# Value-weight products of a fused attention and mixture kernel, moved from one pair of PSUM banks to another

## The chip, the cores and the metric

One core of a Trainium2 chip runs the whole kernel. The metric is device microseconds (us) for one execution of the kernel, median of several runs; lower is better.

## What is computed

Three stages feed each other.

```python
# 1. Nystrom attention: 4 batches, 8 heads, 576 tokens, 64 wide, 32 landmarks
A  = softmax(q @ k_lm.T / 8); Bm = softmax(q_lm @ k_lm.T / 8); C = softmax(q_lm @ k.T / 8)
Z  = iterated inverse of Bm (6 steps Z = 2 Z - Z Bm Z)
x  = A @ Z @ C @ v                       # 2304 tokens x 512
# 2. gated feed-forward, 512 -> 1536 -> 512
xn = x / rms(x) * g
x  = (silu(xn @ w_gate) * (xn @ w_val)) @ w_out
# 3. mixture of 8 experts, one per token, 512 -> 1024 -> 512, on tokens with x @ w_skip > 0
out = x + gate * (relu(x @ w1[e]) @ w2[e])
```

## The kernel before

The attention's result is never formed. `A @ (Z C v)` has only 32 landmark rows per head between `A` and the rest, so the kernel multiplies the small matrix `Z C v` (with the norm's scale, held as `WT`) into the feed-forward's weights first. These products, tiles `P`, are what the change touches: for each batch there are six, the gate's (`g`) and the value's (`v`) weights in three column thirds q = 0, 1, 2. Below (g,1) means the gate's product of third 1. The feed-forward then multiplies `P` with `ap_t` (the attention weights `A`, scaled by the norm).

The tokens go in eight units u = 0 to 7, two halves of each of the four batches. In `run_unit` a unit has twelve blocks f = 0 to 11, each six matmuls `pg` (gate) and six `pv` (value), then 144 matmuls `o` with `w_out`. Blocks 0 to 3 use third 0 of `P`, 4 to 7 third 1, 8 to 11 third 2. `hidden_g` and `hidden_v` turn a block into `h_t`: tanh on ScalarE (ACT), two multiplications on VectorE (DVE), a cast on ACT, and a subtraction on GpSimd (POOL).

Beside a unit, other work is threaded in as Python generators: the next batch's attention (`attention`, `group`: tiles `pb`, `sq`, `cT`, `sk`, small `pv` per group of four heads, then the inverse with tiles `nr`, then `gram`, `sq`, `ms`), its preparation (`prep`: tiles `ap`, `ap_t`, after the norm `rbs`), the products (`products`, `product`), and the last unit's output and routing (`finish`: tiles `lp`, `lg`, `x2t`). The program is then handed to a scheduler, which fixes one order for each engine in advance, using its own estimates of durations and of which buffer is free when. On the chip each engine runs its order strictly, waiting on semaphores.

PSUM has eight banks of 128 x 512 floats in three pools: `acc` has four (`pg`, `pv`, `o`), `pa` has two with the tag `a` (after the first batch, all of the attention takes its banks here, through `atbank`), `pb` has two with the tag `b` (through `bank`: the products and everything of `finish`).

`product` (line 821) takes two banks, runs sixteen matmuls into them, and `rsplit` empties each: one cast on ACT and one subtraction on DVE per bank. The weights come back from HBM in `load_w` (line 781): four transfers of 256 KB per product, issued on SyncE's queue (SP). The gate's land in two buffers `wl`, the value's in two buffers `wr`, so the transfers for the next third wait until the product of the third before has read its buffers:

```python
        for n in "gv":
            product(b, q, n)
            ...
            elif n == "g" and q < NQ - 1:
                load_w(n, q + 1)
```

Of the kernel before, what the change touches and what calls it, by code (L numbers as in the profile page):

```python
# [6 lines left out]
F32 = mybir.dt.float32  # L7
# [55 lines left out]
def attention_moe_kernel(  # L63
# [13 lines left out]
    def pool(stack, name, bufs=1, **kw):  # L77
        return stack.enter_context(tc.tile_pool(name=name, bufs=bufs, **kw))

    def rsplit(lo_eng, hi, lo, src):  # L80

        A.copy(hi, src)
        lo_eng.tensor_tensor(lo, src, hi.bitcast(F32), ALU.subtract)
# [28 lines left out]
    pa = pool(ph1, "pa", bufs=2, space=PSUM)  # L112
# [29 lines left out]
    def bank(name):  # L142
        return pb.tile([128, 512], F32, name=name, tag="b")
# [661 lines left out]
    def ptile(n, g, q):  # L805
        i = PIECES.index((n, g))
        return P_t[q][:, i, 0], P_t[q][:, i, 1]
# [13 lines left out]
    def product(b, q, n):  # L821

        pss = [bank("P") for g in range(2)]
        ws = wparts.pop((n, q))

        with tc.manual_schedule(engines={nc.tensor.engine}):
            for c in (1, 0):  # L830
                for i in range(KC):
                    for g in (1, 0):
                        gs = slice(64 * g, 64 * g + 64)
                        PE.matmul(
                            pss[g][32 * i : 32 * i + 32, PC * c : PC * c + PC],
                            WTs[b][gs, i], ws[c][gs, i], start=True, stop=True,
                        )
        for g, ps in enumerate(pss):
            hi, lo = ptile(n, g, q)
            rsplit(V, hi, lo, ps)  # L840

    def products(b, q):

        if b == 0:
            for n, g in PIECES:
                product0(q, n, g)
                yield
            return
        last = b == B - 1 and q == NQ - 1
        for n in "g" if last else "gv":  # L850
            if (n, q) not in wparts:
                load_w(n, q)
        for n in "gv":
            product(b, q, n)
            if last and n == "g":
                load_w("v", q, last)
                yield
            elif n == "g" and q < NQ - 1:
                load_w(n, q + 1)
            yield  # L860
# [555 lines left out]
```

## Time and profile before

| | us |
|---|---|
| median of 3 runs (711.12 to 711.80) | 711.46 |
| the profiled execution | 710.12 |
| its span, first to last instruction | 708.4 |
| TensorE busy (PE) in the span | 650.1 (92%) |
| VectorE busy (DVE) | 459.8 (65%) |
| ScalarE busy (ACT) | 295.4 (42%) |
| GpSimd busy (POOL) | 145.1 (20%) |

The profiled execution's time lies 1.72 us over its span and 1.34 us under the median. A busy PE is not PE at its peak: the ends of matmuls are modelled, and a stretch at half the granted clock counts as busy too. Sixteen matmuls of a product stand as 32 rows of the trace (`x32`), since each plain float32 matmul leaves two rows; `pg`, `pv` and `o` leave one each. The time after about 500 us is the last unit and the mixture of experts.

### The profile page before, as it was taken

The page shows a single profiled execution, that of the slowest core. Times are in us where ns is not written, and L with a number is a line of the kernel's source. Part 1 is how long each engine was busy: PE and PEld are TensorE (multiplying, and loading weights), DVE is VectorE, ACT ScalarE, POOL GpSimd, SP SyncE. Part 2 cuts the span into 40 slices and gives each one's busy share as a digit, 9 for nine tenths or more (in the row PEclk, how much of TensorE's full clock was granted, in tenths as well). Part 3 has the DMA queues.
Part 4 walks back from the last instruction along what each step waited for, and adds up shares of the span by engine and source line. Part 5 has one row for each costly group of instructions (what it writes and reads, how often), then busy time and mean ns, then how long its engine had stood idle before and what let it go on. Part 6 is the DMA issues. An engine that isn't in the chain of part 4 may idle for free.

```text
span 708.4 us, 13179 instructions
## 1 busy us (share of the span) xinstructions
PE 650.1 (92%) x4895; PEld 561.1 (79%) x4895; DVE 459.8 (65%) x1030; ACT 295.4 (42%) x637; POOL 145.1 (20%) x162
## 2 busy tenths in 40 slices
PE   5368599798998899999999999999989999999997
PEld 5256177687986598978899887999889988988985
DVE  5995999979877596878368768261452554352451
ACT  0873888834324431443341335240452244242340
POOL 4000035213200140220040030040372024022120
PEclk9775799999998999999999999999999999999999
DMA  8686644762238543428522108230451275445454
GB/s 295 229 256 223 218 148 160 215 171 83 67 95 182 123 111 86 132 64 201 134 66 68 66 20 170 67 73 1 161 153 64 60 234 197 150 130 175 134 158 147
DMA packets 79439, 97.17 MB, mean 137 GB/s; under 512 B 16016, under 2 KB 58000, under 8 KB 79376
## 3 DMA queue, kind: packets, MB, share of 16 engines
q1 hardware_dynamic: 79376, 96.33, 46.2%
q8 instruction: 39, 0.64, 0.4%
q14 instruction: 24, 0.20, 0.1%
HBM read 76.97 MB, written 19.34 MB: 136 GB/s over the span
## 4 chain that ended last, share of the span: by engine, by line
PE 70%; DVE 16%; DMA 4%; ACT 3%; issue 3%; POOL 2%; SPq 1%; POOLq 0%; ACTq 0%; DVEq 0%
PE o L58 17%; PE py L58 11%; PE ph L58 11%; PE pv L58 9%; PE pg L58 8%; PE P L58 3%; PE sq L58 3%; DVE wo L58 3%; PE nr L58 2%; DVE h L58 2%; DVE rbs L58 2%; DVE P L58 1%; PE sk L58 1%; DMA kq<-in_q_dram 1%; DVE ap L58 1%
## 5 line engine op out<-in xcount | busy, mean ns | idle before, releaser
L58 PE MATMUL o<-h_t,wo 128*128 128x288 f32 x1152 | 168.1, 301 | 6.5 <-ACT wo L58 3.6
L58 PEld LDWEIGHTS o<-h_t,wo 128*128 128x128 f32 x1152 | 157.3, 190 | 15.5 <-issue 5.9
L58 POOL TENSOR_TENSOR h_t<-h,h_t 128x288 fp32r<-128x288 f32 x96 | 81.6, 853 | 366.1 <-ACT h_t L58 343.8
L58 PE MATMUL pg<-ap_t,P 128*128 128x288 f32 x576 | 101.1, 305 | 10.8 <-ACT P L58 7.9
L58 PE MATMUL pv<-ap_t,P 128*128 128x288 f32 x576 | 102.4, 306 | 2.5 <-DVE h L58 2.1
L58 PEld LDWEIGHTS pg<-ap_t,P 128*128 128x128 f32 x576 | 83.1, 190 | 22.9 <-issue 14.8
L58 PEld LDWEIGHTS pv<-ap_t,P 128*128 128x128 f32 x576 | 83.8, 191 | 8.7 <-DVE h L58 4.3
L58 PE MATMUL ph<-xsh,P 128*128 128x288 f32 x384 | 78.1, 296 | 0.0
L58 DVE SCALAR_TENSOR_TENSOR h<-h,pg 128x288 f32<-128x288 f32 x96 | 42.6, 446 | 33.8 <-ACT h L58 33.2
L58 PEld LDWEIGHTS ph<-xsh,P 128*128 128x128 f32 x384 | 62.0, 188 | 0.6 <-issue 0.5
L58 ACT ACTIVATE h<-pg 128x288 f32<-128x288 f32 x96 | 39.2, 410 | 49.1 <-PE pg L58 46.4
L58 PE MATMUL ph<-xsl,P 128*128 128x288 f32 x192 | 56.9, 296 | 0.0
L58 ACT CAST h_t<-h 128x288 fp32r<-128x288 f32 x96 | 41.2, 431 | 30.2 <-DVE h L58 29.7
L58 PE MATMUL py<-wo,h_t 128*128 128x512 f32 x210 | 51.7, 397 | 0.0
L58 DVE TENSOR_TENSOR h<-h,pv 128x288 f32<-128x288 f32 x96 | 42.5, 446 | 7.7 <-PE pv L58 5.0
L58 PEld LDWEIGHTS py<-wo,h_t 128*128 128x128 f32 x210 | 39.5, 188 | 9.6
L58 DVE STREAM_TRANSPOSE T<-kq 64x576 f32<-64x576 f32 (+1 forms) x40 | 35.5, 887 | 5.1 <-DMA kq<-in_k_dram 4.0
L58 PEld LDWEIGHTS ph<-xsl,P 128*128 128x128 f32 x192 | 36.0, 188 | 0.1
L58 DVE TENSOR_TENSOR P<-P,P 128x512 fp32r<-128x512 f32 x48 | 31.6, 681 | 6.8 <-ACT P L58 6.5
L58 POOL TENSOR_TENSOR P<-w1r,P 128x512 fp32r<-128x512 f32 x16 | 21.2, 1329 | 69.0 <-ACT P L58 66.9
L58 ACT CAST P<-P 128x512 fp32r<-128x512 f32 x48 | 26.3, 587 | 21.7 <-PE P L58 21.1
L58 DVE TENSOR_SCALAR x2T<-o 128x288 f32<-128x288 f32 x16 | 7.3, 456 | 40.6 <-PE o L58 40.5
(235 smaller groups left out, 954.5 us busy)
## 6 DMA issues: line engine op xcount, KB each, us to landing
wl<-wg_d SPq DMA_DIRECT2D x36, 256.0 KB, 4.6
wr<-wv_d SPq DMA_DIRECT2D x32, 256.0 KB, 4.9
w1r<-in_moe_w_dram SPq DMA_DIRECT2D x32, 256.0 KB, 3.3
wr<-in_moe_w_gate_dram SPq DMA_DIRECT2D x6, 1024.0 KB, 6.3
wr<-in_moe_w_val_dram SPq DMA_DIRECT2D x6, 1024.0 KB, 5.9
wo<-in_moe_w_dram SPq DMA_DIRECT2D x24, 256.0 KB, 5.0
kq<-in_k_dram SPq DMA_DIRECT2D x8, 576.0 KB, 4.4
kq<-in_q_dram SPq DMA_DIRECT2D x8, 576.0 KB, 4.1
```

The source lines that it names most:

```text
L58: return f(*args, **kw)
```

## The change

In `product` the value's two banks now come from `pa`, the pool that the attention uses; the gate's still come from `pb`.

```diff
-        pss = [bank("P") for g in range(2)]
+
+        if n == "g":
+            pss = [bank("P") for g in range(2)]
+        else:
+            pss = [pa.tile([128, 512], F32, name="P", tag="a") for g in range(2)]
```

No instruction is added or removed; the scheduler lays the orders out anew, and they differ from the first product of batch 1 (near the end of unit 1) up to unit 6. In the orders below `P<-wl` is a gate's product, `P<-wr` a value's, and `x16` its sixteen matmuls.

The first place is TensorE from the end of unit 1 into unit 2, before:

```order
L58 MATMUL P<-wl,WT 32x256 x16
L58 MATMUL o<-h_t,wo 128x288 x54
L58 MATMUL pg<-ap_t,P_675 128x288
L58 MATMUL P<-wl,WT 32x256 x16
L58 MATMUL pg<-ap_t,P_675 128x288 x5
L58 MATMUL P<-wr,WT 32x256 x16
L58 MATMUL pb<-lmk_2544,bdq 64x32 x2
L58 MATMUL sq<-T,bdq 64x288
L58 MATMUL pv<-ap_t,P_675 128x288 x2
L58 MATMUL pg<-ap_t,P_675 128x288 x5
L58 MATMUL pv<-ap_t,P_675 128x288 x4
```

and with the change:

```order
L58 MATMUL P<-wl,WT 32x256 x16
L58 MATMUL o<-h_t,wo 128x288 x6
L58 MATMUL P<-wr,WT 32x256 x16
L58 MATMUL o<-h_t,wo 128x288 x33
L58 MATMUL P<-wl,WT 32x256 x16
L58 MATMUL o<-h_t,wo 128x288 x15
L58 MATMUL pg<-ap_t,P_675 128x288 x6
L58 MATMUL pv<-ap_t,P_675 128x288 x6
L58 MATMUL pg<-ap_t,P_675 128x288 x6
L58 MATMUL P<-wr,WT 32x256 x16
L58 MATMUL pv<-ap_t,P_675 128x288 x6
```

The product (v,0), which `pv` of block 0 needs, stood after (g,1) and after `pg` of block 0; now it follows (g,0) at once. The attention of batch 2 (`pb`, `sq` and so on), whose first group stood in blocks 0 to 7 of unit 2, now starts in the `o` part of that unit.

The second place is TensorE from unit 3 into unit 4, before:

```order
L58 MATMUL P<-wr,WT 32x256
L58 MATMUL pv<-ap_t,P_984 128x288 x5
L58 MATMUL o<-h_t,wo 128x288 x3
L58 MATMUL P<-wr,WT 32x256 x15
L58 MATMUL o<-h_t,wo 128x288 x28
L58 MATMUL P<-wl,WT 32x256
L58 MATMUL o<-h_t,wo 128x288 x8
L58 MATMUL P<-wl,WT 32x256 x15
L58 MATMUL o<-h_t,wo 128x288 x17
L58 MATMUL P<-wr,WT 32x256
L58 MATMUL o<-h_t,wo 128x288
L58 MATMUL P<-wr,WT 32x256 x15
```

and with the change:

```order
L58 MATMUL pg<-ap_t,P_984 128x288 x4
L58 MATMUL pv<-ap_t,P_984 128x288 x6
L58 MATMUL o<-h_t,wo 128x288 x5
L58 MATMUL ms<-sq,onesd 128x288 x2
L58 MATMUL o<-h_t,wo 128x288 x6
L58 MATMUL P<-wr,WT 32x256 x16
L58 MATMUL o<-h_t,wo 128x288 x4
L58 MATMUL P<-wl,WT 32x256 x16
L58 MATMUL o<-h_t,wo 128x288 x46
L58 MATMUL P<-wr,WT 32x256 x16
```

Products that were cut into one matmul and fifteen now stand whole, and (g,1) follows (v,0) after 4 `o` matmuls in place of 28.

The third place is TensorE from unit 5 into unit 6, before:

```order
L58 MATMUL P<-wr,WT 32x256
L58 MATMUL pg<-ap_t,P_984 128x288 x6
L58 MATMUL pv<-ap_t,P_984 128x288 x2
L58 MATMUL P<-wr,WT 32x256 x15
L58 MATMUL pv<-ap_t,P_984 128x288 x4
L58 MATMUL o<-h_t,wo 128x288 x24
L58 MATMUL P<-wl,WT 32x256
L58 MATMUL o<-h_t,wo 128x288 x7
L58 MATMUL P<-wl,WT 32x256 x15
```

and with the change:

```order
L58 MATMUL pg<-ap_t,P_984 128x288 x3
L58 MATMUL P<-wr,WT 32x256 x16
L58 MATMUL pg<-ap_t,P_984 128x288 x3
L58 MATMUL pv<-ap_t,P_984 128x288 x6
L58 MATMUL o<-h_t,wo 128x288 x16
L58 MATMUL P<-wl,WT 32x256 x16
```

Here too the products stand whole, and (g,1) comes eight `o` matmuls earlier.

## Rows read from the trace of the kernel before

**Rows 1.** Engine busy time by stretch: PE, PEld, DVE, ACT, POOL; granted clock; DMA share, GB/s.

```profile
210.00:220.00 10.00, 8.92 (x90) 7.98 (x89) 9.97 (x17) 4.48 (x10) 0.00 (x0) 1.00 0.59 145
220.00:230.00 10.00, 8.72 (x64) 6.39 (x65) 6.03 (x18) 3.17 (x8) 0.81 (x1) 0.66 1.02 220
230.00:240.00 10.00, 8.85 (x102) 4.89 (x100) 3.23 (x8) 3.92 (x11) 0.81 (x1) 1.00 0.53 116
240.00:250.00 10.00, 8.66 (x107) 6.74 (x107) 9.32 (x22) 4.53 (x14) 1.85 (x2) 1.00 0.48 112
250.00:260.00 10.00, 9.93 (x92) 9.44 (x91) 8.71 (x27) 4.72 (x13) 5.12 (x6) 1.00 0.32 91
```

**Rows 2.** Timeline of PE, units 1 to 2: start, duration, instruction, idle time before it.

```profile
208.42 1.09 PE L58 MATMUL P<-wl,WT 64*32 64x256 f32 x32
...
220.71 2.20 PE L58 MATMUL P<-wr,WT 64*32 64x256 f32 x32 [1.78 <-DVE P L58]
...
236.64 0.62 PE L58 MATMUL P<-wl,WT 64*32 64x256 f32 x2 [0.67 <-DVE P L58]
...
241.79 1.74 PE L58 MATMUL P<-wr,WT 64*32 64x256 f32 x32
...
246.72 0.77 PE L58 MATMUL lg<-ident,h 128*128 128x9 f32 x6 [1.02 <-DVE P L58]
```

**Rows 3.** PE by stretches of one us: busy, granted clock, DMA share, GB/s.

```profile
136.00:137.00 1.00, 1.00 (x7) 0.71 0.14 53
...
139.00:140.00 1.00, 1.00 (x6) 0.59 0.54 169
...
215.00:216.00 1.00, 1.00 (x10) 1.00 0.27 51
...
221.00:222.00 1.00, 1.00 (x25) 0.87 1.00 294
...
228.00:229.00 1.00, 1.00 (x7) 0.71 1.18 226
```

**Rows 4.** Timeline of PE in unit 0.

```profile
124.58 2.22 PE L58 MATMUL o<-h_t,wo 128*128 128x288 f32 x14 [1.46 <-ACT wo L58]
...
135.05 6.04 PE L58 MATMUL o<-h_t,wo 128*128 128x288 f32 x32 [1.79 <-POOL wo L58]
```

**Rows 5.** Timeline of DVE, units 1 to 2.

```profile
208.83 3.76 DVE L58 RECIPROCAL rbs<-rbs 128x288 f32<-128x288 f32 x2
...
219.97 1.28 DVE L58 TENSOR_TENSOR P<-P,P 128x512 fp32r<-128x512 f32 x2
...
222.04 0.44 DVE L58 SCALAR_TENSOR_TENSOR h<-h,pg 128x288 f32<-128x288 f32 x1
```

**Rows 6.** The chain of work that ended last, in order of time: start, us, what.

```profile
230.75 0.80 PE pg L58 x6
...
260.61 15.18 PE o L58 x114
...
344.62 1.02 PE P L58 x32
...
427.92 7.11 DMA wl<-wg_d
...
478.85 19.19 PE o L58 x144
```

**Rows 7.** Timeline of PE, units 3 to 4 and 5 to 6.

```profile
314.19 1.08 PE L58 MATMUL P<-wl,WT 64*32 64x256 f32 x28
...
323.65 0.62 PE L58 MATMUL P<-wl,WT 64*32 64x256 f32 x2
...
425.20 1.08 PE L58 MATMUL P<-wl,WT 64*32 64x256 f32 x28
...
435.16 0.59 PE L58 MATMUL P<-wl,WT 64*32 64x256 f32 x2 [0.45 <-DMA wl<-wg_d]
```

**Rows 8.** Timeline of SP, unit 1: issue of the gate's weights for third 1.

```profile
209.18 3.30 SPq L793 DMA_DIRECT2D wl<-wg_d  x4
```

## The prediction

> **What bounds the kernel now.** I read the busy times first, by stretches. From unit 1 to the end TensorE is the engine that is hardly ever free, so the time is what TensorE has to do plus what it waits or runs slowly. The table by stretches shows where that is: between 210 and 260 us PE is busy 8.92, 8.72, 8.85, 8.66 and 9.93 of 10 us, so it idles 4.9 us there [rows 1]. In the same place the granted clock falls to 0.66 over ten microseconds [rows 1], and VectorE is busy 9.97 of 10 us just before [rows 1].
>
> Then the timeline of PE, to see what it waited for. At 220.71 it starts a value's product after 1.78 us idle, released by DVE emptying a P bank; at 236.64 again, 0.67 us; at 246.72 the routing's `lg` waits 1.02 us for the same kind of bank [rows 2]. So in this place six products and the last unit's output queue for two banks. DVE cannot empty them sooner: from 208.83 it is held by a reciprocal of 3.76 us [rows 5].
>
> After the longest of these waits the clock falls: 0.87 in the us from 221, 0.71 in that from 228 [rows 3]. Read as full speed and half (2.4 and 1.2 GHz), that is half speed from about 221.7 to 228.6, 6.8 us. In unit 0, two idle times close together, the second of 1.79 us [rows 4], are followed by half speed from about 136.4 to 139.8 [rows 3], while a single one of 1.46 us [rows 4] was followed by none. A half-speed stretch costs half of what PE works in it: about 1.7 us for the short one and 3.1 for the long one, less its idle half microsecond.
>
> **The change, part by part.** No instruction comes or goes. At full speed a block half takes 0.80 us [rows 6], a whole product 1.02 [rows 6], an `o` matmul 19.19 / 144 = 0.133 [rows 6], before and after. Only waits, clock and the cutting of products can change.
>
> *Place one, units 1 to 2.* What can be won there: idle 4.9, half speed 3.1, a product stretched by a wait inside it, 1.74 - 1.02 = 0.7, and one cut product, whose single first matmul holds PE 0.62 [rows 2] where a two-row share of 1.02 would be 0.06: 0.55. Together 9.3 us.
>
> What comes in place: (v,0) is now ready when block 0 needs it, so the wait of 1.78 goes. Next late are three things. First, the weights of (g,1). The new order comes to that product after 6 + 33 `o` matmuls and one product: 209.5 (the end of the first product in [rows 2]) + 5.2 + 1.0 = 215.7. SP issues its four transfers from 209.18 to 212.48 [rows 8], and the DMA's share falls to 0.27 in the us from 215 [rows 3], so they have landed at 215.3 when alone; the value's transfers now follow on SP at once and share the DMA. I take 1.2 us of wait (bounds 0 and 2.6; the upper one from the 7.11 us of a shared transfer [rows 6], counted from the last issue, 211.7). Second, VectorE. The first multiplication of `h` stood at 222.04 [rows 5]; now the value's two subtractions, 1.28 us [rows 5], and about 0.5 of landmark sums go ahead of it, so it comes at about 223.9. PE, two blocks ahead by its four `acc` banks, then waits about 1.0 for the block after, since four more subtractions of 0.64 stand between. Third, `lp`, `lg` and `x2t` still share the gate's two banks: 1.7, the larger part of two evacuations, and 0.6 at block 7. Sum of the three: 4.5. Place one gives 9.3 - 4.5 = 4.8. Bounds: 3.1 if VectorE makes all the waits as long as now and only the clock comes back; 8.1 if only the weights' wait remains. The attention group moved into the `o` part of unit 2 costs PE the same there; its DVE work leaves the crowded stretch with it, and if it did not, the 3.3 us of waits on VectorE counted above (1.0, 1.7 and 0.6) would about double.
>
> *Place two, units 3 to 4.* Four products that were cut stand whole: 4 x 0.55 = 2.2 won (one of the four is the 0.62 in [rows 7]). But (g,1) comes earlier: after (g,0), which ends at 315.3 [rows 7], stand 25 `pg`, `pv` and `o` matmuls (3.3), one product and two short `ms`: 5.2 us, where before it was 8.4 (323.65 [rows 7], without a wait). Weights land 5.8 us after the end of (g,0) in place one (215.3 - 209.5) and at most 8.4 here, so PE waits 0.6 to 3.2; I take 1.7, nearer the lower end since the first two transfers can start sooner. Place two gives 0.5 (bounds -1.0 and 1.6).
>
> *Place three, units 5 to 6.* Here PE waited for the weights already, 0.45 us [rows 7], for a transfer of 7.11 us that landed at 435.03 [rows 6]. Eight `o` matmuls (1.1) and a cut product (0.55) leave the way before it, so PE is there at 434.7 - 1.65 = 433.1 and waits 1.9, or 2.7 if the value's transfers, now started sooner, slow it; I take 2.2, that is 1.75 more, less 1.1 for two products that stand whole: -0.7 (bounds -1.5 and 0).
>
> *The clock.* A wait of about 2 us is longer than the one that was followed by half speed [rows 2, 3]. I count one new short half-speed stretch, most likely at place three: -1.7 (bounds 0 and three long ones, 9).
>
> The TensorE page of the Trainium skill (TensorE: Matmul & The Clock Gate, section on a second failure mode, depth-cycling of the PSUM queue) says that many short idles between matmul groups that cycle through banks make the clock swing. By that rule the waits that remain at place one would bring half speed too, 1.7 to 3.1 us, and the time would be 710 to 712. The trace does not bear it out there: between 230 and 250 us PE waited 0.67 and 1.02 us [rows 2] at a granted clock of 1.00 [rows 1].
>
> Sum: 4.8 + 0.5 - 0.7 - 1.7 = 2.9 us less. The profiled execution took 710.12, so 707.2; it stood 1.34 under the median, so 708.6.
>
> **The rivals.**
>
> *VectorE sets place one.* The banks are not the reason, only the place where a full VectorE is felt. For it: 9.97 of 10 us before the stall and the 3.76 us of reciprocals [rows 1, 5]. Against it: in the twenty microseconds of the stall DVE is busy 6.03 and 3.23 of 10 [rows 1]; it waits for PE as much as PE for it. Then place one gives the clock alone, 3.1, less 0.7 and 1.7, and with 0.5: 711.46 - 1.2 = 710.3, or up to 712 with bounds of the other places. The Trainium skill, Perfetto Trace Analysis, section on the most-contended engine, says that VectorE's busy share tells how near it is to its limit and that the most contended engine is the one to relieve. By that rule, with 9.97 of 10 at the start, more banks win nothing; the row shows it for one stretch of ten microseconds and not for the two in which PE waits.
>
> *Half speed at place one as well.* The 4.5 us of waits that remain there come in four pieces within some fifteen microseconds; two idle times close together were enough in unit 0 [rows 3, 4]. That is 1.7 to 3.1 us on top of the sum: 710.3 to 711.7. Against it: the waits of 0.67 and 1.02 us after 230, at full speed [rows 1, 2].
>
> *The weights become the bound (slower).* One mechanism at all three places: with free banks the scheduler puts (g,1) right behind (v,0), before its transfers can have landed. At the upper bounds PE waits 2.6, 3.2 and 2.7 us in place of the 1.2, 1.7 and 2.2 of the sum: 3.4 more; and half speed follows each, three times 1.7 to 3.1 in place of one time 1.7: 3.4 to 7.6 more. That is 715.4 to 719.6. It decides, that is the sum turns negative, when the waits reach about 2.5 us at two places and the clock falls after both. For it: transfers of 7.11 us have been seen [rows 6]. Against it: four of them alone were there 6.1 us after the first issue [rows 3, 8].
>
> *No new half speed, weights nearly in time.* Then 4.8 to 8.1 at place one, and 0 to 1 at the others: 703 to 707.
>
> *The banks of `pa` are taken when the value's products need them.* The attention uses them, so `P` could wait there for `ms` or `sq`. The new order puts (v,0) after `ms`, whose banks are emptied by a short step; I give this little. The time would stay at 711.5.
>
> **How the numbers follow.** A measurement of this kernel can tell about 0.2%, 1.4 us, from no change. Chances: my sum with one new half-speed stretch (706.5 to 710.5) 0.42; no new half speed (703 to 707) 0.22; VectorE, or waits in `pa` (710 to 712.8) 0.14; half speed at place one as well (710.3 to 711.7) 0.07; the weights' waits with half speed at two places or more (712.5 and above) 0.15. Faster than 710.0: 0.40 of the first, all of the second and 0.02 of VectorE's, 0.64; within 0.2%: 0.22; slower: 0.14. The range leaves out the tail of the weights' case above 713 and of the best case below 704: 704.0 to 713.0. Cases of both signs do not share the chance evenly; the likeliest one's own range is 706.5 to 710.5.
>
> **What would show it.** In the changed kernel's profile the `P<-wr` of unit 1 should start without a wait near 210 us, and `pv` of block 0 follow `pg` at once; PE should idle under 4 us between 210 and 250, at a granted clock of 1.00. Near the two later passages, about 5 us after a gate's product ends, a wait of PE `P` for DMA `wl` of 1 to 3 us should stand, and perhaps half speed behind it. The unit's `o` part should start about 13 us earlier in unit 2, of which 5 are the attention group that moved behind. Wrong would be: an idle time at 220 us as long as before (VectorE), no wait for `wl` at all (then the gain is larger), or half speed behind every wait (then it is slower).

## The result and the profile after

The changed kernel takes 703.55 us (median of 11 executions, 699.17 to 706.69); the kernel before, on the same chip, 711.12 us (median of 11, 706.74 to 712.82). The ratio is 0.9891 with an interval of 0.9869 to 0.9912: 7.6 us less. The forecast was 708.6, with 704.0 to 713.0 as its range: right in sign, less than half of the gain, and the time lies 0.45 us under the range. Executions of one kernel differ by about 1% here, so single times below carry little; ratios do.

| us | before | after |
|---|---|---|
| profiled execution | 710.12 | 704.67 |
| span | 708.4 | 702.8 |
| PE busy | 650.1 | 643.6 |
| DVE busy | 459.8 | 459.7 |
| start of (g,0), batch 1 | 208.42 | 211.00 |
| from that start to the end of (g,0), batch 2 | 106.85 | 100.56 |
| from that end to the end of (g,0), batch 3 | 111.01 | 110.35 |
| from that end to the end of the span | 282.12 | 280.89 |

Up to 208 us the two programs are the same; that this stretch took 2.6 us longer in the profile after is the spread between executions. From the first changed product on, the changed kernel needs 8.2 us less: 6.3 around place one, 0.7 around place two, 1.2 around place three and after it. The two small shares are no larger than what these stretches differ by between executions: the middle one took 109.6 us when the change was run again, and the last one 281.5 and 283.8 us in two experiments that keep all the banks of before.

Over place one PE's busy time (then its granted clock, DMA share, GB/s) is, before and after:

```profile
208.42:315.27 106.85, 101.94 (x940) 0.97 0.46 116
211.00:311.55 100.55, 96.38 (x939) 1.00 0.48 117
```

So only 0.7 of the 6.3 us is idle time, 4.9 to 4.2. The other 5.6 are matmuls that take less time: by the prediction's working 3.1 of it is the half speed that is gone, and the products' own busy time falls from 11.2 to 8.6 us, partly by the clock and partly because they stand whole.

The stretches that answer to [rows 1], in the same columns:

```profile
210.00:220.00 10.00, 8.98 (x118) 7.22 (x124) 9.49 (x14) 4.05 (x8) 0.00 (x0) 1.00 0.73 153
220.00:230.00 10.00, 9.92 (x121) 8.54 (x110) 9.31 (x24) 5.77 (x11) 0.81 (x1) 1.00 1.13 245
230.00:240.00 10.00, 7.73 (x101) 5.82 (x109) 5.38 (x14) 4.07 (x12) 2.05 (x3) 1.00 0.57 139
240.00:250.00 10.00, 9.21 (x87) 8.57 (x65) 7.66 (x22) 4.88 (x12) 4.35 (x6) 1.00 0.44 101
```

The clock of 0.66 is gone; it is 1.00 throughout. PE still idles about 4.2 us from 210 to 250, a little over the 4 that the prediction named as a sign. But VectorE, at 9.49 and 9.31 of 10 us where it was 9.97 and 6.03, now works through the stretch in which it stood waiting before. What PE waits for stands in its timeline (the rows that answer to [rows 2, 7]):

```profile
211.00 1.09 PE L58 MATMUL P<-wl,WT 64*32 64x256 f32 x32
213.02 1.09 PE L58 MATMUL P<-wr,WT 64*32 64x256 f32 x32
219.73 1.22 PE L58 MATMUL P<-wl,WT 64*32 64x256 f32 x32 [1.02 <-DVE P L58]
...
230.24 1.06 PE L58 MATMUL pv<-ap_t,P 128*128 128x288 f32 x6 [0.32 <-DVE h L58]
...
233.78 0.69 PE L58 MATMUL lp<-x2T,wcat 128*32 128x288 f32 x8 [1.46 <-DVE P L58]
235.05 0.77 PE L58 MATMUL lg<-ident,h 128*128 128x9 f32 x6 [0.57 <-ACT h L58]
...
243.97 1.07 PE L58 MATMUL pg<-ap_t,P 128*128 128x288 f32 x6 [0.79 <-DVE h L58]
...
310.90 0.66 PE L58 MATMUL P<-wl,WT 64*32 64x256 f32 x14
...
318.72 1.10 PE L58 MATMUL P<-wl,WT 64*32 64x256 f32 x32 [1.14 <-DMA wl<-wg_d]
...
420.83 1.08 PE L58 MATMUL P<-wl,WT 64*32 64x256 f32 x28
...
429.39 1.22 PE L58 MATMUL P<-wl,WT 64*32 64x256 f32 x32 [0.69 <-DMA wl<-wg_d]
```

At 213.02 the value's product (v,0) follows without a wait where it stood at 220.71 after 1.78 us of idle time [rows 2]. The waits that remain at place one add up to 1.02 + 0.32 + 1.46 + 0.57 + 0.79 = 4.16 us; places two and three have the waits for the gate's weights that were forecast, shorter.

The wait of 1.02 us before (g,1) is put down to VectorE emptying a `P` bank. What VectorE had just emptied were the value's banks, which (g,1) doesn't use. It had done with the gate's at 217.66 (timeline of DVE in the changed kernel, first line below), and when the change was run again the same wait was put down to the weights (timeline of PE in that run, second line). So it is read here as the wait for the weights that was forecast.

```profile
216.98 0.68 DVE L58 TENSOR_TENSOR P<-P,P 128x512 fp32r<-128x512 f32 x1
...
218.40 1.22 PE L58 MATMUL P<-wl,WT 64*32 64x256 f32 x32 [1.45 <-DMA wl<-wg_d]
```

### The profile page after: what moved, and what is told of

Read it like the earlier page. It is cut to its first block, busy times and chain, and to the rows that moved or that the text cites. A ratio compares the mean times of both kernels' runs of the same rounds, so it can differ in the third digit from the quotient of the medians.

```text
span 702.8 us, 13190 instructions
## 1 busy us (share of the span) xinstructions
PE 643.6 (92%) x4895; PEld 559.6 (80%) x4895; DVE 459.7 (65%) x1030; ACT 296.5 (42%) x637; POOL 145.1 (21%) x162
## 4 chain that ended last, share of the span: by engine, by line
PE 72%; DVE 15%; ACT 4%; DMA 3%; issue 3%; POOL 1%; SPq 1%; POOLq 0%; ACTq 0%; DVEq 0%
PE o L58 18%; PE py L58 11%; PE ph L58 11%; PE pv L58 9%; PE pg L58 8%; PE sq L58 3%; PE P L58 3%; DVE wo L58 2%; DVE h L58 2%; DVE rbs L58 2%; DVE P L58 2%; PE nr L58 2%; PE sk L58 2%; DMA kq<-in_q_dram 1%; DVE ap L58 1%
## 5 line engine op out<-in xcount | busy, mean ns | idle before, releaser
L58 PE MATMUL pv<-ap_t,P 128*128 128x288 f32 x576 | 100.5, 303 | 3.5 <-DVE h L58 3.0
L58 DVE SCALAR_TENSOR_TENSOR h_t<-ph,h_t 128x288 fp32r<-128x288 f32 (+2 forms) x45 | 14.6, 352 | 28.4 <-ACT h_t L58 28.4
```

The costliest lines, as they stand in the source:

```text
L58: return f(*args, **kw)
```

## The experiments

**Where the gain is: batch 1 alone.** The value's products take the attention's banks for batch 1 only, which is place one.

```diff
-        if n == "g":
+        if n == "g" or b != 1:
```

> The value's products use the attention's banks for batch 1 alone; batches 2 and 3 keep the shared pair. The orders are those of the change up to unit 2, and close to those of before from unit 4 on. If place one holds nearly all of the gain (6.3 of 8.2 us by the traces from the first product of batch 1 on), this is 5 to 7 us faster than before, ratio 0.990 to 0.993, and the passages from unit 3 to 4 and 5 to 6 take 27.7 and 28.4 us as before. If the gain is spread over the places as products that stand whole, it is about a third: 2 to 3 us, ratio 0.996 to 0.997.

Measured: 704.8 us (median), ratio 0.9921 (0.9893 to 0.9948). The stretch at place one takes 100.62 us, against 100.56 with the whole change. So most of the gain is place one: 5.6 of 7.7 us by the ratios, whose intervals overlap. In its timeline of PE the waits there are those of the change, that of `lp` for one:

```profile
231.58 0.69 PE L58 MATMUL lp<-x2T,wcat 128*32 128x288 f32 x8 [1.45 <-DVE P L58]
```

**The rest alone: batches 2 and 3.**

```diff
-        if n == "g":
+        if n == "g" or b == 1:
```

> The counterpart: the attention's banks for batches 2 and 3 alone. The place of the 1.78 us wait is as before. If place one holds the gain: 1 to 2.5 us faster than before, ratio 0.9965 to 0.9985. If whole products at the later passages are worth as much as place one: 3 us or more, ratio under 0.996. By the weights rival it would be slower than before.

Measured: 711.18 us, ratio 1.0028 (0.9997 to 1.0059): nothing won, where 1 to 2.5 us were expected. In its timeline of PE the wait at place one is back, and at place three the weights are 2.15 us late, as the forecast had it there:

```profile
220.87 2.55 PE L58 MATMUL P<-wr,WT 64*32 64x256 f32 x32 [1.76 <-DVE P L58]
...
327.86 0.94 PE L58 MATMUL o<-h_t,wo 128*128 128x288 f32 x5 [1.31 <-POOL h_t L58]
...
434.24 1.22 PE L58 MATMUL P<-wl,WT 64*32 64x256 f32 x32 [2.15 <-DMA wl<-wg_d]
```

Its stretches (columns as in [rows 1]) show half speed after the first of these waits and none after the last, though that one is longer:

```profile
220.00:230.00 10.00, 8.92 (x76) 6.44 (x77) 6.20 (x18) 3.42 (x8) 1.62 (x2) 0.83 0.95 213
...
430.00:440.00 10.00, 7.85 (x84) 7.03 (x82) 8.90 (x15) 4.92 (x10) 1.38 (x2) 1.00 1.05 211
```

**Order without banks.** The kernel before gets (v,0) behind (g,0) by its generators alone; all products keep one pair of banks.

```diff
         for n in "gv":
             product(b, q, n)
...
-            yield
+            if n == "v":
+                yield
```

> The kernel before with its one pair of banks, but the value's product of a third is written right after the gate's, so that (g,1) no longer stands ahead of (v,0) in unit 2. This is the order without the banks. If the order was what cost the 1.78 us wait and the half speed after it, it gains 4 to 7 us with two banks, ratio 0.990 to 0.994. If the banks are the reason, the wait moves to another product: 0 to 2.5 us, ratio 0.9965 to 1.0, and PE still idles 4 us or more between the first product of batch 1 and the end of unit 2's blocks.

Measured: 712.67 us, ratio 1.0023 (0.9992 to 1.0053). In its timeline of PE the wait at 220 us is gone, and a longer one stands further on: the routing's `lp` waits for a bank behind the products that now come earlier.

```profile
235.59 1.10 PE L58 MATMUL P<-wr,WT 64*32 64x256 f32 x32
242.13 1.19 PE L58 MATMUL lp<-x2T,wcat 128*32 128x288 f32 x8 [5.45 <-DVE P L58]
```

Half speed sets in during that wait (clock, third column from the end):

```profile
240.00:250.00 10.00, 7.87 (x59) 7.05 (x60) 7.80 (x19) 2.23 (x9) 1.16 (x1) 0.53 0.49 145
```

This fits a queue for two banks in which the order only chooses who waits. It is one other order; that no order does better with two banks isn't shown.

**The weights made late.** The change, with the gate's next weights issued after the value's product. The edit does one thing more, which was not intended: it fetches one third's weights twice. Its profile counts 40 transfers `wl<-wg_d` of 256 KB where the change has 36, and eight of them, in place of four, are issued between (g,1) and (g,2) at place one. The first four for (g,1) are issued as early as in the change (211.59 against 211.77).

```diff
-            elif n == "g" and q < NQ - 1:
-                load_w(n, q + 1)
+            elif n == "v" and q < NQ - 1:
+                load_w("g", q + 1)
```

> The change, with the gate's weights for the next third fetched only after the value's product, behind the value's own transfers on the queue. TensorE's order is nearly that of the change. PE's waits for these weights, 1.14 and 0.69 us in the changed kernel, should grow by 1.5 to 3 us at each of three places. If waits of 2 us or more bring half speed, as I forecast, each costs 1.7 to 3.1 us more: 8 to 15 us slower than the change, 1 to 8 slower than before. If they do not, 4 to 8 us slower than the change, about the time of before.

Measured: 709.76 us, ratio 0.9992 (0.9963 to 1.0021): the whole gain is gone. One wait in its timeline of PE does most of it:

```profile
234.55 2.08 PE L58 MATMUL P<-wl,WT 64*32 64x256 f32 x32 [3.39 <-DMA wl<-wg_d]
```

and its stretches show half speed behind it (columns as in [rows 1]); with the 3.39 us this makes place one 5.7 us longer than in the change (106.26 against 100.56):

```profile
230.00:240.00 10.00, 4.52 (x48) 2.34 (x48) 1.33 (x3) 2.13 (x5) 0.80 (x1) 0.72 1.08 257
240.00:250.00 10.00, 10.00 (x86) 9.09 (x87) 8.13 (x25) 4.58 (x14) 2.40 (x3) 0.76 0.44 119
```

At the other places the waits for these weights are 1.27 (place one, third 1), 0.28 and 1.25 us: the growth of 1.5 to 3 us that was expected at each place didn't come. Weights that land late can cost the whole gain, then. But the long wait stands behind a megabyte that the change doesn't fetch, so this run doesn't show that the order of issue alone would do it. In the change the transfers come in time to keep the waits small.

**VectorE relieved, without new banks and with them.** Four subtractions of batch 1's `ap_t` go to GpSimd, which is idle there; once in the kernel before, once in the changed one.

```diff
-            rsplit(V, ap_t[:, half, g, 0], ap_t[:, half, g, 1], a)
+            rsplit(eng, ap_t[:, half, g, 0], ap_t[:, half, g, 1], a)
...
-            prep(1)
+            prep(1, G if u == 2 else None)
...
-                    prep(0)
+                    prep(0, G if u == 1 else None)
```

> The banks of before (all products in one pair), but the four subtractions of batch 1's ap_t, 1.7 us by their rows, leave VectorE for GpSimd, which stands idle there. Theory of the banks: the order still puts the value's product of third 0 behind the gate's of third 1, and its banks come free when VectorE has emptied them; that can come at most 1.7 us sooner, so the wait of 1.78 us shrinks or goes, the half speed behind it perhaps with it, and the wait of lg for a bank stays. Gain 0 to 4.8 us, well short of the 7.6 of the change. Theory of VectorE (full in the ten microseconds before the wait, and the banks only where that is felt): with VectorE relieved the whole gain comes without new banks, 703 to 705 us.

Measured: 709.69 us, ratio 1.0 (0.9974 to 1.0026). The kernel before gains nothing that can be measured. Its timeline of PE:

```profile
217.24 1.22 PE L58 MATMUL P<-wl,WT 64*32 64x256 f32 x32
221.31 1.69 PE L58 MATMUL P<-wr,WT 64*32 64x256 f32 x32 [1.20 <-DVE P L58]
224.08 0.31 PE L58 MATMUL pb<-lmk,bdq 128*64 128x32 f32 x4 [1.08 <-DVE bdq L58]
...
245.04 0.77 PE L58 MATMUL lg<-ident,h 128*128 128x9 f32 x6 [1.31 <-DVE P L58]
```

The wait before (v,0) falls from 1.78 to 1.20 us, `pb` and `lg` wait longer, and half speed now sets in after `lg` (granted clock 0.56 in the us from 246). But the edit didn't do what it was meant to. VectorE begins to empty the banks of (g,1) 2.1 us after that product ends (220.58, against 217.24 + 1.22), where it was 1.9 us before (219.97 [rows 5], against 218.06), since it first waits for GpSimd and then does the landmark sums `s` (timeline of DVE):

```profile
218.31 2.01 DVE L58 TENSOR_TENSOR s<-T 128x576 f32<-128x576 f32 x2 [0.74 <-POOL ap_t L58]
...
220.58 1.27 DVE L58 TENSOR_TENSOR P<-P,P 128x512 fp32r<-128x512 f32 x2
```

The wait is shorter only because PE has 1.7 us of other work behind (g,1) in place of 0.9. So this run doesn't settle the rival that VectorE sets place one. What speaks against it is the change itself: VectorE's busy time is the same, 459.8 and 459.7 us, and with two more banks place one is 6.3 us shorter. A kernel in which VectorE empties the two shared banks sooner was not run.

> The change, and the four subtractions of batch 1's ap_t on GpSimd as well. Theory of the banks: of the waits that the change leaves at place one, VectorE's h sets 0.32 and 0.79 us and the emptying of P banks 1.02 and 1.46; 1.7 us less of VectorE's work ahead of them takes away 0 to 1.5 us: 702.0 to 703.5. Theory of VectorE: it is what still sets place one (busy 9.49 and 9.31 of 10 us from 210 and 220), so all 3.6 us of waits that end on it go: 700 us or less.

Measured: 704.18 us, ratio 0.9923 (0.9895 to 0.9952): as the change, and short of both expectations. In its timeline of PE, of the waits on VectorE `lp`'s shrinks from 1.46 to 0.86 us and those for `h` go. But the weights of (g,1) come later: PE is there 6.6 us after (g,0) ended, as in the change, and starts it after 9.1 us, where it was 7.6:

```profile
218.57 2.08 PE L58 MATMUL P<-wl,WT 64*32 64x256 f32 x32 [2.49 <-DMA wl<-wg_d]
...
233.93 0.69 PE L58 MATMUL lp<-x2T,wcat 128*32 128x288 f32 x8 [0.86 <-DVE P L58]
```

By its stretches the clock falls behind that wait, and once more behind the two of 0.86 and 0.57 us before 236:

```profile
210.00:220.00 10.00, 7.51 (x98) 6.26 (x99) 8.85 (x12) 3.00 (x7) 2.38 (x3) 0.93 1.02 206
220.00:230.00 10.00, 10.00 (x105) 8.72 (x90) 6.99 (x19) 5.24 (x11) 1.63 (x2) 0.90 0.88 215
230.00:240.00 10.00, 8.57 (x82) 7.05 (x81) 4.52 (x11) 3.78 (x11) 1.61 (x2) 0.83 0.41 99
```

**The pairs swapped.** The gate's products in the attention's pair, the value's in the pair of the routing.

```diff
-        if n == "g":
+        if n == "v":
```

> The pairs swapped: the gate's products take the attention's two banks, the value's share theirs with the routing. Theory of two pairs: it counts only that gate and value do not queue for the same banks, so 702 to 705.5 us, with the value's product of third 0 right behind the gate's and no wait ahead of it; lp then no longer stands behind the gate's product of third 2. Rival: the attention's pair must be the value's, because the gate's products, which come first, would now wait for ms or sq or hold them up: 707 us or more.

Measured: 697.52 us, ratio 0.9823 (0.9798 to 0.9848). It beats both kernels, and the change by more than was expected. Its timeline of PE:

```profile
209.16 1.45 PE L58 MATMUL P<-wl,WT 64*32 64x256 f32 x32
211.53 1.09 PE L58 MATMUL P<-wr,WT 64*32 64x256 f32 x32
...
218.72 1.22 PE L58 MATMUL P<-wl,WT 64*32 64x256 f32 x32 [1.50 <-DMA wl<-wg_d]
...
227.61 0.69 PE L58 MATMUL lp<-x2T,wcat 128*32 128x288 f32 x8 [0.40 <-DVE P L58]
...
428.49 1.22 PE L58 MATMUL P<-wl,WT 64*32 64x256 f32 x32
```

`lp` comes before (g,2), so its wait falls from 1.46 to 0.40 us; `lg` and `x2t` stand late in unit 2 and wait for nothing; no wait for `h` is left at place one; and at place three (g,1) stands behind 52 `o` matmuls, so that its weights are there.

**`lp` and `lg` to the attention's pair.**

```diff
-        lp = bank("lp")[:, 0:NH]
+        lp = pa.tile([128, 512], F32, name="lp", tag="a")[:, 0:NH]
...
-        lg = bank("lg")
+        lg = pa.tile([128, 512], F32, name="lg", tag="a")
```

> The change, and lp and lg of the routing in the attention's pair too, so that at place one lp no longer waits for the gate's banks of third 2 (1.46 us) nor lg behind it (0.57). If these waits just go: 701.5 to 702.5 us. Rival: lp and lg now queue with the value's products and the attention in the same two banks, and the waits come back there, in this unit or another: 703 to 706 us.

Measured: 707.72 us (702.70 to 714.72), ratio 0.9979 (0.9951 to 1.0008): worse than the change, and than both expectations. Its profiled execution, with a span of 700.9 us, was the fastest of the twelve; in its timeline of PE `lp` waits 0.33 us at place one, and at place three the weights are waited for longer than in the change:

```profile
425.96 1.22 PE L58 MATMUL P<-wl,WT 64*32 64x256 f32 x32 [1.59 <-DMA wl<-wg_d]
```

What costs the other executions some 5 us this profile doesn't show; it stays open.

**The swap for batch 1 alone.** Batches 2 and 3 as in the change.

```diff
-        if n == "g":
+        if n == ("v" if b == 1 else "g"):
```

> The pairs swapped for batch 1 alone (gate's products in the attention's pair there, value's as in the change for batches 2 and 3). In the profiles the swapped kernel stands 2.5 us before the change at place one, 0.8 in unit 4 and 1.3 in unit 6. If these are separate effects of the banks: 2.5 us of the 4.6 stay, so 700 to 702, with lp's wait at place one 0.4 in place of 1.46 and no waits of pg and pv for h there. Rival: the better part of the gain comes with batches 2 and 3, or from the spread between executions: 702.5 to 704.5, as the change.

Measured: 700.32 us, ratio 0.9857 (0.9820 to 0.9894), beside the change's 0.9876 on the same chip (below). In its profile the way from the start of the `o` part of unit 1 to that of unit 2 takes 61.56 us, against 64.18 in the change run beside it: 2.6 us less, where 2.5 were expected at place one. From the `o` part of unit 5 to that of unit 6 it takes 46.88 us, as the change (46.83), where the full swap takes 45.51. By the profiles the swap's parts are separate effects; by the ratios alone, whose intervals overlap, that isn't settled.

**Two queues for the weights.** The swap, with half of (g,1)'s weights issued on ScalarE's queue.

```diff
-                SP.dma_start(
+                (nc.scalar if (n, q, c) == ("g", 1, 1) else SP).dma_start(
```

> The pairs swapped, and two of the four transfers of the gate's weights for third 1 issued on ScalarE's queue beside SP's two. In the swapped kernel the product (g,1) waits 1.50 us for them at place one; SP takes 3.55 us to issue the four. If the issue on one queue is what makes them late, they land about 1.5 us sooner and the wait at place one goes: 695.5 to 697, though the order is laid out anew and (g,1) stands nine o matmuls earlier, which takes 1.2 us of that back. Rival: the DMA's rate sets the landing (its share is 1.0 to 1.1 while they run), or ScalarE, held by the issue, is late with its own work: 697.5 to 701.

Measured: 709.97 us, ratio 0.9987 (0.9958 to 1.0017): the whole gain of the swap is lost. The weights come no sooner, 9.3 us after the end of (g,0) (207.0 + 1.45 = 208.4 to 217.73) where it was 8.1 with one queue, while PE, by its new order, comes sooner (timeline of PE):

```profile
206.95 1.45 PE L58 MATMUL P<-wl,WT 64*32 64x256 f32 x32
...
217.73 2.08 PE L58 MATMUL P<-wl,WT 64*32 64x256 f32 x32 [3.92 <-DMA wl<-wg_d]
...
433.09 1.22 PE L58 MATMUL P<-wl,WT 64*32 64x256 f32 x32 [2.77 <-DMA wl<-wg_d]
```

By stretches of one us (columns as in [rows 1]) the DMA's share is over 1 from 210 on, at some 200 to 290 GB/s. With a second queue the value's transfers begin sooner too, 2.0 us after the gate's first in place of 3.7 (timeline of the queues), and share that rate. The clock falls while PE still waits.

```profile
216.00:217.00 1.00, 0.00 (x0) 0.00 (x0) 1.00 (x2) 0.00 (x0) 0.00 (x0) 0.57 1.14 201
217.00:218.00 1.00, 0.27 (x8) 0.30 (x16) 0.13 (x1) 0.00 (x0) 0.00 (x0) 0.50 1.14 228
```

**The change again.**

> The change itself, beside the two others on one chip, so that the swapped pairs can be compared with it there. Both theories: 702 to 705 us. In its profile again no stretch at half the clock between 205 and 480 us, and waits of 1.0 to 1.5 us at place one.

Measured: 701.94 us, ratio 0.9876 (0.9840 to 0.9913), as the first time. No stretch between 205 and 480 us is at a lower clock, and place one takes 100.66 us.

## Why the prediction was right, and where it wasn't

**The mechanism was right, the sum was not.** Six products and the routing queued for two banks; a second pair lets (v,0) start when block 0 needs it. Another order with two banks gains nothing (ratio 1.0023), and the banks for batch 1 alone (0.9921) come near to the whole change (0.9891). The case that came was the rival without new half speed, 703 to 707, to which 0.22 was given. The likeliest case, with 0.42, failed in three terms: a wait of 2.2 us at place three, which came out at 0.69; a stretch of half speed behind it, 1.7 us, which didn't come; and place one, where 1.2 us more could be won than the 9.3 that were counted.

| term | forecast, us won | measured in the profiles |
|---|---|---|
| place one | 4.8 | 6.3 |
| place two | 0.5 | 0.7 |
| place three | -0.7 | 1.2 |
| one new half-speed stretch | -1.7 | 0 |
| sum | 2.9 | 8.2 |

The measured shares of places two and three lie within the spread between executions, as said above, and the run with batches 2 and 3 alone shows no gain (1.0028).

**Place three was mis-sized by 1.9.** That PE would be there at 433.1, 6.8 us after (g,0) ended, was right: it came 429.39 - 0.69 - 421.91 = 6.8 us after. The wait of 1.9 to 2.7 us at that point was not: it took the landing from the kernel before, 8.75 us after (g,0), and in the change (g,1) could start 7.5 us after. The wait is 0.69 in place of 2.2, and the term becomes 1.1 - 0.24 = 0.9. For the change it came out at 0.69, and at 0.65 when it was run again. In the experiment with batches 2 and 3 alone, with the same banks at this place and PE there after the same 6.8 us, it is 2.15. What makes the weights land 1.5 us sooner or later these runs don't show.

The landing was misread at place one too. The DMA's share falls in the us from 215 [rows 3], but in the same trace the last of the four transfers lands 4.8 us after its issue, at about 216.6: 7.1 us after (g,0) and not 5.8, and 7.4 us after the first issue and not 6.1. In the change (g,1) starts 7.6, 7.2 and 7.5 us after (g,0) at the three places.

**The clock was mis-sized by 1.7.** "A wait of about 2 us is longer than the one that was followed by half speed" fell with its premise: the longest wait in the changed parts is 1.46 us. It would have been weak even so, by the waits in the last section. Nor do the runs show why waits of up to 1.46 us at place one bring none: in six profiles with two pairs there and no wait over 1.50 us none does, while in the kernel with less VectorE work two shorter ones did.

**Place one was mis-sized by 1.5.** The waits that take the place of the old ones were forecast as 4.5 and are 4.16; (g,1) waits 1.02 where 1.2 was put, `lp` and `lg` 2.03 where 1.7 was put, and the waits for `h` are 1.11 where 1.6 was put. So the error is in what could be won, 6.3 + 4.2 = 10.5 and not 9.3. One step that failed is "the attention group moved into the `o` part of unit 2 costs PE the same there". By groups of instructions (busy us, mean ns of one), before, from 221 to 251.6 us, in the blocks of unit 2:

```profile
L58 PE MATMUL sq<-T,bdq 128*64 128x288 f32 x8 | 2.4, 493 | 0.0
L58 PE MATMUL sk<-T,bdk 128*64 128x288 f32 x8 | 1.9, 425 | 0.0
```

and after, from 252 to 270 us, in its `o` part:

```profile
L58 PE MATMUL sq<-T,bdq 128*64 128x288 f32 x8 | 1.2, 419 | 0.0
L58 PE MATMUL sk<-T,bdk 128*64 128x288 f32 x8 | 1.2, 419 | 0.0
```

In the blocks these were cut in two by other work, and a part of `sq` ran at half speed, some 0.6 us that the sum had counted. Whole, they take 1.9 us less, 1.3 of it not counted. But the group now cuts the `o` matmuls in its turn. Over place one these are busy 29.47 us where they were 28.14. Busy times overlap where one tile's matmuls follow another's; with each us counted once, an estimate from the two timelines, `sq`, `sk` and `cT` take 1.7 us less beyond the clock and `o` 0.9 more. That leaves about 0.8 of the missing 1.2. A second item was in no term: (v,0) itself, 2.20 us before [rows 2], was stretched by a wait inside it for its second bank. About 0.6 of its length is neither its own 1.02 nor half speed. Both are estimates from one profile each, and no experiment took them apart.

**Place two** held in size: 2.2 less the wait for the weights, which is 1.14 in place of 1.7 (0.34 when run again); 1.1 by that, 0.7 measured, within the spread.

**The rules that were weighed.** The Trainium skill (TensorE: Matmul & The Clock Gate, section on a second failure mode, psum-queue depth-cycling) would have brought half speed to the short waits left at place one. In the change's two profiles four to five waits of 0.3 to 1.46 us stand there at a granted clock of 1.00; the rule doesn't hold for them. In the kernel with less VectorE work it may: there the clock fell near 236 us, after waits of 0.86 and 0.57 us. The Trainium skill (Perfetto Trace Analysis, Identifying the Most-Contended Engine) would have relieved VectorE first, if it is read for the ten microseconds before the stall. Four subtractions fewer on it gave a ratio of 1.0, in a run in which it came to the banks no sooner; two more banks, with VectorE's work as before, gave 0.9891.

## What to carry to other kernels

When products with different consumers share a pair of PSUM banks, the wait is shown on the engine that empties them, though here the cure was a second pair. Taking four subtractions off that engine won nothing, and in the other order that was tried another consumer waited longer. Two assignments of the same banks can differ by 0.5 to 0.7% (0.9823 against 0.9876 and 0.9891, each against the kernel before on its own chip), since they also decide who stands behind whom; try both, and see in each profile which wait is late next. Cost a moved group of small matmuls by its rows in the new neighbourhood, not the old one: cut by other work, `sk` takes 1.9 us for 1.2. Count what it cuts there as well: `o` is busy 1.3 us more.

## What was not expected of the hardware

The length of a wait didn't tell whether half speed follows. Around place one it set in within or soon after waits of 1.31, 1.76, 1.78, 2.49, 3.39, 3.92 and 5.45 us, and not after others of 1.02 to 1.50 us; at place three waits of 2.15 and 2.77 us were followed by none. What sets the two places apart these runs don't show.

A second issuing queue didn't bring transfers sooner where the DMA's share was already over 1: the product that waits for four transfers of 256 KB started 9.3 us after the one that frees their buffers, in place of 8.1.
